# Sliding-window attention and an MLP on one core: the overflow guard's flag is summed where its counts land, without an order behind the residual add of tile 22

## The chip, the cores and the metric

One core of a Trainium2 chip runs the whole kernel. The metric is the time of one launch on the device in microseconds (us), the median of the runs shown. The engines that matter are TensorE (PE, with PEld for its weight loads), VectorE (DVE), ScalarE (ACT), GpSimd (POOL) and SyncE (SP). A name with a q behind it in the profile (POOLq, SPq) is that engine's sequencer: it loads registers, branches, waits on semaphores and issues DMAs.

## The reference

Inputs are q, k and v of 4 batches, 8 heads, 768 positions and 64 values per head, in float32. Cut to what matters:

```python
scores = q @ k.T / 8
keep = (column < 4) | ((0 <= row - column) & (row - column < 128))   # 4 sinks, a window of 128
a = softmax(where(keep, scores, -1e9))
x = (a @ v), heads side by side                    # (4, 768, 512)
xn = (x - mean) / sqrt(var + 1e-6) * g_ln
out = x + relu(xn @ w_ch1) @ w_ch2                 # 512 -> 2048 -> 512
```

## The kernel before

The 4 x 768 rows are 24 tiles of 128 rows (`NT = 24`), and two tiles make a chunk of 256 rows (`NC = 12`). A chunk's attention gives `x`, which is normalised, transposed by a DMA that SP issues (L598), multiplied by `w1` (`mlp`, matmuls on L1070), put through a ReLU on ACT (L1081), and multiplied by `w2`. From chunk 3 on the second product is done block by block with seven products of halves instead of eight (`second_by_seven`, matmuls on L1122); for this DVE makes sums and differences of halves of the hidden layer (L1098, tiles named `sb` and `natc`). The last chunk, tiles 22 and 23, has its own code (`last_by_seven`): its DVE additions are on L1174 and its stores on L1179. The names of those additions in the code are k11, k21, k22, o11, o21, o22, k12 and o12; the table `tail["sum", t]` keeps, for a tile, one operation of its residual sum. For tile 22 (`NT - 2`) that is the operation named o21.

The softmax is done without subtracting the maximum. A guard says whether that was allowed. On DVE it clamps the reciprocals of all sums, compares the clamped ones with the originals and counts, for each of the 128 partitions, how many differ (L1285 to L1287, into `n_bad`). A DMA that POOL issues (L1291, `gmove`) turns the column of 128 counts into a row on one partition (`n_bad_t`). DVE then sums the row (L1295, into `n_sum`) and converts the sum to an integer (L1296, into `flag`); these two instructions are the operation `gflag`. At the end each of the five engines loads `flag` into a register (L1335) and branches on it (L1337): where it is zero, each jumps over a slow general version of the whole computation (`general`). After the branch stands the end of the program (shown under L1372): the engines wait for what is outstanding, meet at a barrier that POOL collects, clear the semaphores, and meet once more.

What sets the order is a planner (`Plan`). Every operation is given with its engines and assumed costs, the buffers that it reads and writes, and a priority (a smaller number goes first). `Plan.run` goes through an imagined time, and on each engine it starts the operation with the best priority among those that could start within a short window; the instructions are written out in the order of those start times. `after=[...]` makes an operation start only when the listed ones have ended. `gflag` has priority 1000, behind all other work of DVE. The last store on SP (`order_last`) is kept back and written behind SP's load of the flag, the other engines' loads of the flag stand behind everything else that they do:

```python
bad = nc.values_load(flag, min_val=0, max_val=128 * NT * H)
order_last.emit(order_last.eng)
```

Two operations named `hold` and `hold_act` (L1299, L1302) make PE and ACT read the last output value before they load the flag.

Of the kernel before, what the change touches and what calls it, by code (L numbers as in the profile page):

```python
# [213 lines left out]
def fix(occ, extra=0.09):  # L214
    return (occ, occ + extra)
# [159 lines left out]
def kernel(  # L375
# [23 lines left out]
    NT = B * RB  # L399
# [8 lines left out]
    P = Plan()  # L408
# [110 lines left out]
    def negs(e):  # L519
# [18 lines left out]
         writes=[gr_b], dma=HW_T)  # L538
    P.op("gtt", pe(0.1), PAR["gtt"], lambda e: nc.tensor.transpose(gt_p.t[:, 0:NDM], g_rows, ident_f[0:NDM, 0:NDM]),
         reads=[gr_b, Bc["ident_f"]], writes=[gt_p])  # L540
    P.op("gtc", {"DVE": fix(0.07)}, PAR["gtt"] + 0.1, lambda e: V.tensor_copy(gt, gt_p.t[:, 0:NDM]), reads=[gt_p], writes=[Bc["gt"]])
    for h in range(H):
# [3 lines left out]
            reads=[Bc["vc"]], writes=[Bc["vcd"]], nb=3.5 + 0.55 * h)  # L546
    for b in range(B):
# [4 lines left out]
            reads=[Bc["vcd"], Bc["vc"], Bc["sel4" if b else "sel"]], writes=[Bvs[b]], nb=PAR["vs0"][1] if b == 0 else PAR["vs1"] if b == 1 else 40.0 * b)  # L552
# [8 lines left out]
    for c in range(4):  # L561
        for n in range(len(Bw1[c])):
# [3 lines left out]
                 writes=[Bw1[c][n]], dma=half_w if len(Bw1[c]) > 1 else SW_W)  # L566
    for c in range(4):
        P.op(f"w2ld{c}", {"POOL": (0.75, 0.8)}, PAR["w2p"][c], lambda e, c=c: G.dma_start(
            w2[c], moe_w_ch2[512 * c:512 * (c + 1), :].rearrange("(t p) n -> p t n", p=128)),
            writes=[Bw2[c]], dma=SW_W)  # L570
# [674 lines left out]
    last_use, tail = {}, {}  # L1245
# [19 lines left out]
    for n, (in0, in1, op, reads) in enumerate((  # L1265
# [4 lines left out]
        for m in range(2):  # L1270
            P.op(f"w2t{n}{m}", {"DVE": dve(1024, 0.64), "POOL": (2.1, 2.2)} if PAR["w2t_pool"] else {"DVE": dve(1024, 0.64)}, 16.0 * PAR["seven"] + PAR["w2t"] + 0.5 * n + 0.1 * m,
                 lambda e, n=n, m=m, in0=in0, in1=in1, op=op: (V if e == "DVE" else G).tensor_tensor(w2t[n][m], in0(m), in1(m), op=op),
                 reads=[Bw2[m], Bw2[m + 2], *reads], writes=[Bw2t[n]], after=natf_users if n < 2 else natp_users)
    for c in range(NC):
        mlp(c)
        if c == PAR["x_by_dma"] - 1:
            for s in range(4):
                for j in range(NDM):
# [3 lines left out]
                         reads=[*Bw1[s], Bc["gt"]], writes=[Bw1g[s]], after=last_use[s])  # L1282

    def guard(e):
# [3 lines left out]
    nb_b, fl_b = Buf("n_bad"), Buf("flag")  # L1288
    P.op("guard", {"DVE": fix(0.9)}, 1000.0, guard, reads=recs, writes=[nb_b])
    nt_b = Buf("n_bad_t")  # L1290
    P.op("gmove", {"POOL": (0.8, 0.85)}, 1000.0, lambda e: G.dma_start(n_bad_t[0:1, :], n_bad[:, 0:1]),  # L1291
         reads=[nb_b], writes=[nt_b], dma=SW_Q)

    def total(e):
        V.tensor_reduce(out=n_sum, in_=n_bad_t, op=ALU.add, axis=mybir.AxisListType.X)  # L1295
        V.tensor_copy(flag, n_sum)  # L1296
    P.op("gflag", {"DVE": fix(0.2)}, 1000.0, total, reads=[nt_b], writes=[fl_b], after=[tail["sum", NT - 2]])
    hl = Buf("hold", "one")
    P.op("hold", pe(0.06), 1000.0, lambda e: nc.tensor.matmul(  # L1299
        hl.t[0:1, 0:1], lhsT=tail["ot"].t[:, tail["at"]:tail["at"] + 1], rhs=ones_f, start=True, stop=True),  # L1300
        reads=[tail["ot"], tail["oo"], Bc["ones_f"]], writes=[hl])
    P.op("hold_act", {"ACT": act(1)}, 1001.0, lambda e: nc.scalar.copy(act_end, tail["ot"].t[0:1, tail["at"]:tail["at"] + 1]),  # L1302
         reads=[tail["ot"], tail["oo"]], writes=[Buf("hold_act")])
# [73 lines left out]
```

## Time and profile before

| | us |
|---|---|
| median of 3 runs | 209.81 |
| lowest and highest run | 209.40 and 209.91 |
| the profiled execution's own time | 209.76 |
| its span, first to last instruction | 208.2 |
| PE busy in the span | 201.3 (97%) |
| DVE busy in the span | 160.7 (77%) |
| POOL busy in the span | 115.7 (56%) |

Between the span and the time of the profiled execution lie 1.56 us, before the first and behind the last instruction that the trace shows. Positions are given in us from the start of the span. PE's granted clock is full in all 40 slices of the page. Rows that group instructions by line give the smallest, median and longest duration in nanoseconds, and then the start of the first and of the last instruction of the group.

### The profile page before, as it was taken

Reading aid. Unit: us, or ns where it says so; the run is one execution under the profiler, and the core shown is the slowest. Engines: PE = TensorE matmul, PEld = TensorE weight load, DVE = VectorE, ACT = ScalarE, POOL = GpSimd, SP = SyncE. Lnnn points to the kernel's source line nnn. Section 1 sums busy time; section 2 is a strip of 40 time slices with the busy share of each in tenths; the row PEclk is TensorE's granted clock in tenths of the full one; section 3 lists DMA queues with packets and bytes.
Section 4 is the critical chain, followed back from the end, with each engine's and each line's share of the span. In section 5 each row is a group of like instructions: output and inputs, shape, how many; then the busy total and the mean of one; then the engine's idle time right before and its main releaser. Section 6 shows DMA issues by size and latency. Waiting matters only on the chain.

```text
span 208.2 us, 7258 instructions
## 1 busy us (share of the span) xinstructions
PE 201.3 (97%) x2987; PEld 169.9 (82%) x2987; DVE 160.7 (77%) x434; ACT 120.8 (58%) x216; POOL 115.7 (56%) x170
## 2 busy tenths in 40 slices
PE   7798999999999999999999999999999999999993
PEld 2457985688889888888888888888888888888892
DVE  5599764899948889888788788888788788772483
ACT  3798786343675499575565564565564564463520
POOL 7969842479799794848767666567442022320000
PEclk9999999999999999999999999999999999999999
DMA  5999999999999799999999999999997310310403
GB/s 151 191 186 199 190 205 206 172 181 148 141 201 130 74 184 156 76 196 160 82 203 125 104 196 125 107 199 107 124 187 61 126 28 5 126 28 0 104 13 98
DMA packets 103789, 27.56 MB, mean 132 GB/s; under 512 B 92740, under 2 KB 100936, under 8 KB 103752
## 3 DMA queue, kind: packets, MB, share of 16 engines
q0 software_dynamic: 70960, 13.18, 90.9%
q1 hardware_dynamic: 31448, 13.09, 35.8%
q10 hardware_dynamic: 1344, 0.79, 1.3%
q8 instruction: 24, 0.39, 0.9%
q14 instruction: 13, 0.11, 0.2%
HBM read 27.43 MB, written 6.29 MB: 162 GB/s over the span
## 4 chain that ended last, share of the span: by engine, by line
PE 91%; DVE 3%; DMA 3%; ACT 1%; issue 1%; ACTq 0%
PE one L1070 41%; PE one L1122 27%; PE one L1228 10%; PE pair L1011 3%; DMA natf<-in_q_dram 3%; PE one L984 2%; PE one L991 2%; PE one L1000 1%; PE one L927 1%; PE pair L1019 1%; DVE st L905 1%; DVE x L897 1%; PE pair L626 1%; PE pair L754 1%; PE one L882 0%
## 5 line engine op out<-in xcount | busy, mean ns | idle before, releaser
L1070 PE MATMUL one<-xnt,w 128*128 128x256 bf16 x768 | 88.5, 273 | 0.3 <-issue 0.3
L1070 PEld LDWEIGHTS <-w 128*128 128x128 bf16 x768 | 74.0, 98 | 10.0 <-issue 0.5
L1081 ACT ACTIVATE h<-one 128x512 bf16<-128x512 f32 x86 | 51.3, 598 | 35.9 <-PE one L1070 34.3
L667 POOL DMA_DIRECT2D vn<-in_v_dram x59 | 39.2, 689 | 8.3 <-DMA w<-in_moe_w_ch_dram 7.1
L1029 ACT ACTIVATE pe<-pair 128x768 bf16<-128x768 f32 x36 | 27.2, 809 | 16.5 <-PE pair L1011 16.0
L915 POOL TENSOR_SCALAR st<-st 128x1 f32<-128x1 f32 x24 | 9.6, 401 | 48.0 <-DVE st L907 47.6
L1122 PEld LDWEIGHTS <-h 128*128 128x128 bf16 x224 | 21.4, 98 | 2.6 <-issue 0.2
L1228 PE MATMUL one<-w,h 128*128 128x256 bf16 (+1 forms) x160 | 22.9, 294 | 0.0
L1228 PEld LDWEIGHTS <-h 128*128 128x128 bf16 x160 | 15.1, 98 | 4.6
L1122 PE MATMUL one<-w,h 128*128 128x256 bf16 (+1 forms) x152 | 18.8, 267 | 0.0
L1122 PEld LDWEIGHTS <-sb 128*128 128x128 bf16 x176 | 16.9, 98 | 2.2
L1129 ACT COPY tx<-one 128x256 f32<-128x256 f32 x24 | 9.0, 375 | 16.2 <-PE one L1122 16.2
L916 POOL TENSOR_TENSOR st<-st,mhalf 128x1 f32<-128x1 f32 x24 | 16.6, 691 | 2.0
L905 DVE BATCH_NORM_STATS2 st<-x 128x6 f32<-128x512 bf16 x24 | 16.7, 694 | 0.8
L1163 DVE TENSOR_TENSOR ot<-ot,x 128x512 f32<-128x512 f32 x15 | 10.4, 692 | 7.6 <-ACT ot L1129 7.4
L1054 DVE TENSOR_TENSOR x<-one,rec 128x256 bf16<-128x256 f32 x36 | 15.2, 422 | 1.1
L727 POOL DMA_DIRECT2D nat<-in_k_dram x16 | 14.9, 935 | 1.4 <-DMA natp<-in_q_dram 1.4
L727 POOL DMA_DIRECT2D nat<-in_q_dram x16 | 14.4, 910 | 0.0
L919 DVE TENSOR_SCALAR xc<-x,st 128x512 bf16<-128x512 bf16 x18 | 7.4, 412 | 7.5 <-POOL st L916 7.5
L1122 PE MATMUL one<-natf,sb 128*128 128x256 bf16 x92 | 12.5, 273 | 0.0
L1034 DVE TENSOR_TENSOR pe<-pe,band 128x768 bf16<-128x768 bf16 x24 | 11.9, 538 | 0.0
L1122 PEld LDWEIGHTS <-natc 128*128 128x128 bf16 x112 | 10.6, 98 | 1.4
(148 smaller groups left out, 304.7 us busy)
## 6 DMA issues: line engine op xcount, KB each, us to landing
out_dram<-ot SPq DMA_DIRECT2D x20, 256.0 KB
w<-in_moe_w_ch_dram POOLq DMA_DIRECT2D x6, 512.0 KB, 12.3
nat<-in_k_dram POOLq DMA_DIRECT2D x16, 128.0 KB, 4.7
nat<-in_q_dram POOLq DMA_DIRECT2D x16, 128.0 KB, 5.6
vn<-in_v_dram POOLq DMA_DIRECT2D x44, 32.0 KB, 4.8
w<-in_moe_w_ch_dram POOLq DMA_DIRECT2D x4, 256.0 KB, 11.2
vn<-in_v_dram POOLq DMA_DIRECT2D x15, 64.0 KB, 4.3
natp<-in_k_dram POOLq DMA_DIRECT2D x3, 256.0 KB, 12.1
```

Source lines behind the costliest of these rows:

```text
L667: P.op(f"vld{t}_{i}", {"POOL": (0.8, 0.85)}, prio + 0.001 * i, lambda e, p0=p0, n=n, hs=hs, src=src: G.dma_start(m.t[p0:p0 + n, hs, 0:64], ...
L727: lambda e, nat=nat, ap=ap: G.dma_start(nat.t, ap), writes=[nat], dma=SW_N, after=gate(c), nb=PAR["k_nb"].get((c, nm, i), 0.0))
L905: P.op(f"bn{t}", {"DVE": fix(0.60)}, d + 0.12, lambda e: V.bn_stats(st.t[:, 8:14], x.t), reads=[x], writes=[st, mv])
L916: G.tensor_tensor(st.t[:, 16:17], st.t[:, 17:18], mhalf, op=ALU.pow)),
L1029: nc.scalar.activation(pes[j].t.rearrange("p a b -> p (a b)")[:, 0:768].rearrange("p (a b) -> p a b", a=2), pps[j].t[:, :, 0:384], AF.Exp, ...
L1034: V.tensor_mul(at_s, at_s, band[j] if r > 1 else edge[r][j].unsqueeze(1).to_broadcast([128, 4, 192]))
L1054: P.op(f"x{t - 1}{u}", {"DVE": dve(256)}, d + 0.051 + 0.002 * u, lambda e, u=u, rc=rc, pv=pv: V.tensor_tensor(x.t[:, 256 * u:256 * u + 256 ...
L1070: nc.tensor.matmul(ph.t[:, 256 * s:256 * s + 256], lhsT=w1[ht // 4][:, j, 128 * (ht % 4):128 * (ht % 4 + 1)], rhs=xnt.t[:, j, :], start=j ...
L1081: nc.scalar.activation(dst, ph.t, AF.Relu)
L1122: nc.tensor.matmul(bank.t[:, 0:n], lhsT=left[p](m)[:, a, :], rhs=right[p](m)[:, a, cols], start=new and m + a == 0, stop=m + a == 4, skip_ ...
L1163: V if e == "DVE" else G).tensor_tensor(ot[i].t, ot[i].t, x.t, op=ALU.add), reads=[ot[i], *oo[i], x], writes=[done])
L1228: nc.tensor.matmul(pc.t[:, part], lhsT=h1[s].t[:, 256 * ii + 128 * i:256 * ii + 128 * i + 128], rhs=w2[s][:, ii, sl.start + part.start:sl. ...
```

## The change

The operation `gflag` loses its `after`. Nothing else is edited.

```diff
     def total(e):
         V.tensor_reduce(out=n_sum, in_=n_bad_t, op=ALU.add, axis=mybir.AxisListType.X)
         V.tensor_copy(flag, n_sum)
-    P.op("gflag", {"DVE": fix(0.2)}, 1000.0, total, reads=[nt_b], writes=[fl_b], after=[tail["sum", NT - 2]])
+    P.op("gflag", {"DVE": fix(0.2)}, 1000.0, total, reads=[nt_b], writes=[fl_b])
```

The planner puts the two instructions elsewhere on DVE; on PE, ACT, POOL and SP every instruction stands where it stood. In the rows below a name is a tile with its number, the last figure is partitions x elements.

On DVE, in the middle of chunk 10's second product, among the sums of halves of its hidden layer, the flag's two instructions come in:

```order
@@ -397,4 +397,6 @@
 L1098 TENSOR_TENSOR sb_158<-natc_70,h_150 128x512
 L1098 TENSOR_TENSOR sb_160<-h_152,sb_158 128x512
+L1295 TENSOR_REDUCE n_sum<-n_bad_t 1x1
+L1296 CAST flag<-n_sum 1x1
 L1098 TENSOR_TENSOR natc_72<-h_151,h_153 128x512
 L1098 TENSOR_TENSOR sb_159<-natc_72,h_151 128x512
```

They now stand ahead of the sums that use the hidden halves `h_151` and `h_153`. On DVE, near the end, in the last chunk's additions (`tx` and `ot` are its partial sums and output tiles), they go:

```order
@@ -419,6 +421,4 @@
 L1174 TENSOR_TENSOR tx_167<-one_65,tx_167 128x256
 L1174 TENSOR_TENSOR ot_171<-one_64,tx_167 128x256
-L1295 TENSOR_REDUCE n_sum<-n_bad_t 1x1
-L1296 CAST flag<-n_sum 1x1
 L1174 TENSOR_TENSOR ot_171<-one_65,tx_166 128x256
 L1174 TENSOR_TENSOR tx_164<-one_65,x_122 128x256
```

Behind o21 (`ot_171<-one_64,tx_167`) now comes o22 (`ot_171<-one_65,tx_166`) at once, and then k12.

## The prediction

> **What bounds the kernel now.** I read the page's head first, then its chain of waits, and then, since the edit touches a few tenths of a microsecond, the instructions in order of time around the old and the new place and every row of the program's end.
>
> ```profile
> span 208.2 us, 7258 instructions
> PE 201.3 (97%) x2987; PEld 169.9 (82%) x2987; DVE 160.7 (77%) x434; ACT 120.8 (58%) x216; POOL 115.7 (56%) x170
> PE 91%; DVE 3%; DMA 3%; ACT 1%; issue 1%; ACTq 0%
> ```
>
> The second line is the busy time of the engines, the third the chain that ended last, by engine. TensorE is the bound. An edit on DVE counts only where PE waits for DVE, or behind PE's last product, where the end is made. The profiled execution took 209.76 us, 0.05 under the median of 209.81, so a difference found in its trace is taken off the median as it stands.
>
> The last chunk's end in order of time (start, duration, engine, line):
>
> ```profile
> 202.50 0.42 DVE L1174 TENSOR_TENSOR ot<-one,tx 128x256 f32<-128x256 f32 x1 [0.45 <-PE one L1122]
> 202.73 0.60 PE L1122 MATMUL one<-natf,sb 128*128 128x256 bf16 x4
> 202.84 0.26 DVE L1295 TENSOR_REDUCE n_sum<-n_bad_t 1x1 f32<-1x128 f32 x1
> 202.95 2.39 SPq L1179 DMA_DIRECT2D out_dram<-ot  x2
> 203.13 0.14 DVE L1296 CAST flag<-n_sum 1x1 int32<-1x1 f32 x1
> 203.37 0.42 DVE L1174 TENSOR_TENSOR ot<-one,tx 128x256 f32<-128x256 f32 x1
> 203.60 0.60 PE L1122 MATMUL one<-w,natc 128*128 128x256 bf16 x4
> 204.04 0.61 PE L1122 MATMUL one<-w,h 128*128 128x128 bf16 x8
> 204.24 0.74 DVE L1174 TENSOR_TENSOR ot<-one,tx 128x256 f32<-128x256 f32 x2
> ```
>
> The flag's two instructions run from 202.84 to 203.27. The addition behind them, o22 at 203.37, uses the product whose last matmul ends at 202.73 + 0.60 = 203.33. The two additions at 204.24 follow products that end at 204.20 and 204.65, and the last output is ready at 204.24 + 0.74 = 204.98. So DVE waits for PE here, and the flag lies in that wait.
>
> Now the flag's way out. These are its loads by POOL, SP and ACT, then POOL's steps behind its branch, each group with its duration in ns and its first and last start:
>
> ```profile
> L1335 POOLq TENSOR_LOAD <-flag x1: 502/502/502, 203.3 to 203.3; - x1
> L1335 SPq TENSOR_LOAD <-flag x1: 529/529/529, 203.3 to 203.3; - x1
> ...
> L1335 ACTq TENSOR_LOAD <-flag x1: 498/498/498, 205.1 to 205.1; - x1
> ```
>
> ```profile
> L1337 POOLq EVENT_SEMAPHORE  x5: 17/43/43, 204.4 to 204.7; - x5
> L1337 POOLq COMPARE_BRANCH  x1: 59/59/59, 203.9 to 203.9; - x1
> L1337 POOLq INC_SWDGE_SEM  x1: 632/632/632, 204.8 to 204.8; - x1
> ```
>
> And the end of the program up to the first barrier, which POOL collects, with the release of SP behind it from a later cut of the same view:
>
> ```profile
> L1372 SPq EVENT_SEMAPHORE  x11: 28/28/28, 206.0 to 206.7; - x11
> L1372 SPq DRAIN  x2: 7/10/13, 206.8 to 206.8; - x2
> L1372 POOLq DRAIN  x1: 1865/1865/1865, 205.5 to 205.5; - x1
> L1372 DVEq DRAIN  x1: 17/17/17, 206.0 to 206.0; - x1
> L1372 PEldq DRAIN  x1: 8/8/8, 206.2 to 206.2; - x1
> L1372 ACTq DRAIN  x1: 8/8/8, 206.3 to 206.3; - x1
> L1372 POOLq EVENT_SEMAPHORE  x1: 17/17/17, 207.4 to 207.4; - x1
> ```
>
> ```profile
> L1372 SPq EVENT_SEMAPHORE  x2: 17/17/17, 207.5 to 208.1; - x2
> ```
>
> This is what the chain of waits does not show, since it ends with ACT's last copy. DVE, PE and ACT are through at 206.0, 206.2 and 206.3, SP at 206.8. POOL is last: its drain runs from 205.5 for 1.865 us, its wait for the others ends at 207.4 without waiting for any of them, and SP is let go at 207.5. POOL had nothing else to do since the counts' DMA at 182.93. Its way is flag written at 203.27, load 203.3 to 203.8, branch 203.9, semaphores from 204.4, the counter instruction of 0.632 at 204.8, drain, 207.4: 4.1 us behind the flag. The other four depend on the last output at 204.98 instead. So the flag, by way of POOL, sets the end.
>
> **The change part by part.** *The old place on DVE.* 0.26 + 0.14 and the 0.03 between them, 0.43 us of work, goes. o22 still has to wait for the product that ends at 203.33, and its 203.37 stays; so do the two last additions and 204.98. Worth 0 on the path; late next is PE, as before.
>
> *The new place on DVE.* It is in chunk 10's second product. The rows around it, with the DMA that brings the counts, the ReLU that DVE waits for and the products that follow:
>
> ```profile
> 182.93 0.66 POOL L1291 DMA_DIRECT2D n_bad_t<-n_bad  x1 [0.26 <-DVE n_bad L1287]
> 185.25 0.42 DVE L1098 TENSOR_TENSOR sb<-h,sb 128x512 bf16<-128x512 bf16 x1
> 185.46 0.60 ACT L1081 ACTIVATE h<-one 128x512 bf16<-128x512 f32 x1 [0.28 <-PE one L1070]
> 186.09 0.42 DVE L1098 TENSOR_TENSOR natc<-h,h 128x512 bf16<-128x512 bf16 x1 [0.41 <-ACT h L1081]
> 186.54 0.42 DVE L1098 TENSOR_TENSOR sb<-natc,h 128x512 bf16<-128x512 bf16 x1
> 187.00 1.04 PE L1122 MATMUL one<-natf,sb 128*128 128x256 bf16 x8
> 187.88 1.04 PE L1122 MATMUL one<-w,h 128*128 128x256 bf16 x8
> ```
>
> ```profile
> DMA to landing us min/median/max: 2.0/2.0/2.0
> ```
>
> The counts land 2.0 us after 182.93, at 184.9, 0.7 us before DVE gets there. The sum needs nothing of the instruction ahead of it, and as at 202.50 and 202.84 it can start 0.34 behind that one's start: 185.59, converted by 186.02. Then DVE waits for the ReLU, which ends at 185.46 + 0.60 = 186.06, and goes on at 186.09 as before: the cover is DVE's idle 0.41. If the sum starts only when the work ahead ends (185.67), it is done at 186.10 and the next addition slips by some 0.05. Behind it in DVE's queue stand `natc` and `sb`; `sb` is ready at 186.96 and feeds the second half of the product that starts at 187.00, that is its fifth matmul, at 187.00 + 4 x 0.11 = 187.44 (eight take 187.88 - 187.00). That leaves 0.44 more. With all cover gone the cost would be the whole 0.43, which still fits in it. I take 0, with 0 to 0.43 as bounds.
>
> *SP.* Its flag load cannot move: the store ahead of it is issued at 202.95 and an issue takes 0.342,
>
> ```profile
> L1179 SPq DMA_DIRECT2D out_dram<-ot x3: 332/342/348, 201.3 to 205.0; - x3
> ```
>
> so SP comes to the flag at 203.29 and already loads it at 203.3. Its last store, at 205.0, waits for the output of 204.98. SP's arrival stays at 206.8. DVE, PE and ACT load the flag behind their last work, as before: 0.
>
> *POOL.* With the flag at 186.0 instead of 203.27, POOL's whole way starts 17.2 us earlier: load 186.1, drain from 188.2, at the barrier by 190.2, some 16 us ahead of everyone. It is queued behind nothing, and nobody waits for it until the barrier. Then SP is last, at 206.8. POOL's wait would end there plus the time in which a semaphore passes between engines; the release at 207.5 behind the 207.4 bounds that at 0.1. So the end comes forward by 207.4 - 206.8 - 0.1 = 0.5. Upper bound: SP's whole wait at this barrier, the longest in this row, less nothing:
>
> ```profile
> SPq L1372 <- PEq L1372: 1.2, 2, 0.7
> ```
>
> Lower bound: 0, if the drain's 1.865 us does not move. I take 0.5, since all other steps of POOL's way have durations of their own and only that one is open.
>
> The sum: 0 + 0 + 0 - 0.5. 209.81 - 0.5 = 209.31; for the profiled execution a span of 207.7 and 209.26.
>
> **The rivals.** *B: POOL's drain is tied to the end, and nothing changes.* For it: the drains of the other engines take 8 to 17 ns, POOL's a hundred times that, so it may be a wait for something of the end. In the last 2.5 us the instruction queue moves 4 of the 13 packets of the execution:
>
> ```profile
> q14 instruction: 4, 0.03, 5.0%
> ```
>
> ```profile
> q14 instruction: 13, 0.11, 0.2%
> ```
>
> If POOL's drain waits for such a fetch, and the fetch for what the other engines do once they have the flag, the drain would end at 207.4 in any case: 209.8. Against it: POOL passes its own branch at 203.9, 1.2 us before ACT loads the flag, and the drain follows an instruction that took 0.632 on POOL alone. The Trainium skill ("VectorE: DVE Perf Modes", The DRAIN you can't avoid) says that drains of the start and end code are constant, about 12 ns, on all five engines. By that rule POOL's 1865 ns would be no work of its own, and case B would give 209.8; the rows of four engines agree with it and POOL's does not, so I leave it the smaller chance.
>
> *C: the counts land late and DVE stalls ahead of PE's operands; slower.* DVE is in order, and the three sums behind the flag would wait for the DMA. With a landing at L, the sum starts at L + 0.04, the next addition at L + 0.52 instead of 186.09; with the 0.44 of room PE loses L - 186.01. Set against the 0.5 at the end, the kernel gets slower once the landing comes 3.6 us after the issue, and by over 0.3% at 4.2 us. The landing in this trace took 2.0. POOL's other DMAs take longer, under load and with 64 times the bytes:
>
> ```profile
> vn<-in_v_dram POOLq DMA_DIRECT2D x44, 32.0 KB, 4.8
> ```
>
> At 4.8 us L is 187.73, PE loses 1.7, and the time is 209.81 + 1.7 - 0.5 = 211.0. Against it: POOL issues no load behind 182.93, so the queue is empty.
>
> *D: the cover at the new place fails altogether and the end does not move.* 0.43 more, 210.24, still within 0.3% of before.
>
> **How the numbers follow.** About 0.3% (0.63 us) is what a measurement of this kernel can tell from no change. Case A, the forecast, has 0.71; B 0.14; C 0.09; D 0.06. A's gain lies between 0.4 and the 0.7 of SP's wait, and the runs shown spread by 0.5 us, so I give a third of A to a gain over 0.63: 0.24, and with a little of B's scatter 0.25. Within 0.3%: the rest of A, B and most of D, 0.64. Slower: C and a part of D, 0.11. The range runs from 209.81 - 0.7 less 0.15 of scatter, 208.95, to B's median with the upper half of the spread, 209.95; it leaves out C and D. A alone spans 209.0 to 209.55.
>
> **What would show it.** Right: POOL's flag load near 186.1 and its 1.865 us drain near 188; POOL's barrier wait ending within 0.1 of SP's last drain, at 206.9; DVE's `natc` still at 186.09 and o22 at 203.37; a span near 207.7. Wrong for case A: a POOL drain that lasts to 207.4 or is stretched over the 17 us, or an SP that arrives later than 206.8 because its last store lands later. Wrong for the zero at the new place: a DVE gap ahead of L1295 that ends with the counts' DMA, and PE idle before 187.44.

## The result, and the profile after

The changed kernel takes 209.05 us (median of 9 runs, 208.91 to 209.49), the kernel before 209.64 us (9 runs, 209.31 to 209.95). The ratio is 0.9976, with a 95% interval of 0.9965 to 0.9987: 0.5 us, or 0.24%, faster.

The profiled execution of the changed kernel took 209.49 us, the highest of its runs. The head of its page and its chain of waits:

```profile
span 208.0 us, 7258 instructions
PE 202.2 (97%) x2987; PEld 170.5 (82%) x2987; DVE 161.2 (77%) x434; ACT 120.8 (58%) x216; POOL 115.8 (56%) x170
PE 90%; DVE 4%; DMA 2%; ACT 1%; issue 1%; SPq 0%; ACTq 0%; DVEq 0%
```

The span is only 0.2 us shorter than before, because this execution lost 0.33 us long before the edit: compared matmul by matmul, the two traces are 0.01 us apart at the 500th, at 38.7 us, and 0.31 to 0.34 from the 600th, at 45.7, to the end. So positions here are to be read 0.33 to 0.34 us later than the same work before. The new place, in order of time:

```profile
183.27 0.66 POOL L1291 DMA_DIRECT2D n_bad_t<-n_bad  x1 [0.26 <-DVE n_bad L1287]
185.59 0.42 DVE L1098 TENSOR_TENSOR sb<-h,sb 128x512 bf16<-128x512 bf16 x1
185.93 0.27 DVE L1295 TENSOR_REDUCE n_sum<-n_bad_t 1x1 f32<-1x128 f32 x1
186.24 0.14 DVE L1296 CAST flag<-n_sum 1x1 int32<-1x1 f32 x1
186.42 0.42 DVE L1098 TENSOR_TENSOR natc<-h,h 128x512 bf16<-128x512 bf16 x1
187.34 1.04 PE L1122 MATMUL one<-natf,sb 128*128 128x256 bf16 x8
```

The sum starts 0.34 us behind the start of the instruction ahead of it, the flag is written at 186.38, and `natc` follows at 186.42, which is the 186.09 of before plus the shift. The row of the product still has its eight matmuls in 1.04 us. The old place, with the last output:

```profile
203.70 0.42 DVE L1174 TENSOR_TENSOR ot<-one,tx 128x256 f32<-128x256 f32 x1 [0.45 <-PE one L1122]
204.58 0.74 DVE L1174 TENSOR_TENSOR ot<-one,tx 128x256 f32<-128x256 f32 x2
```

o22 at 203.70 is the 203.37 of before plus the shift: where the flag's 0.43 us stood, DVE now idles 0.45 us until PE is ready. POOL's load of the flag and its steps behind it, and the end up to the first barrier:

```profile
L1335 POOLq TENSOR_LOAD <-flag x1: 502/502/502, 186.4 to 186.4; - x1
...
L1335 SPq TENSOR_LOAD <-flag x1: 532/532/532, 203.7 to 203.7; - x1
```

```profile
L1372 SPq DRAIN  x2: 7/10/13, 207.1 to 207.2; - x2
L1372 POOLq EVENT_SEMAPHORE  x2: 17/17/17, 207.2 to 207.3; - x2
L1372 POOLq DRAIN  x1: 1865/1865/1865, 188.6 to 188.6; - x1
L1372 DVEq DRAIN  x1: 17/17/17, 206.4 to 206.4; - x1
L1372 PEldq DRAIN  x1: 8/8/8, 206.6 to 206.6; - x1
L1372 ACTq DRAIN  x1: 8/8/8, 206.6 to 206.6; - x1
```

POOL's drain has moved to 188.6 and still takes 1.865 us. SP's last drain, at 207.2, is now the last to arrive, and POOL sees it at 207.2. From the last output to the end of the span it is 208.0 - 205.32 = 2.7 us; before it was 208.2 - 204.98 = 3.2. The 0.33 us lost early and this 0.5 make up the whole difference of the spans: 208.16 + 0.33 - 0.50 = 207.99.

### The profile page after: what moved, and what is told of

The parts are those of the page before. It is cut to its first block, busy times and chain, and to the rows that moved or that the text cites. A ratio compares the mean times of both kernels' runs of the same rounds, so it can differ in the third digit from the quotient of the medians.

```text
span 208.0 us, 7258 instructions
## 1 busy us (share of the span) xinstructions
PE 202.2 (97%) x2987; PEld 170.5 (82%) x2987; DVE 161.2 (77%) x434; ACT 120.8 (58%) x216; POOL 115.8 (56%) x170
## 4 chain that ended last, share of the span: by engine, by line
PE 90%; DVE 4%; DMA 2%; ACT 1%; issue 1%; SPq 0%; ACTq 0%; DVEq 0%
PE one L1070 41%; PE one L1122 27%; PE one L1228 10%; PE pair L1011 3%; DMA natf<-in_k_dram 2%; PE one L984 2%; PE one L991 2%; PE one L1000 1%; DVE st L905 1%; DVE x L897 1%; PE one L927 1%; PE pair L1019 1%; DVE xc L912 1%; PE pair L626 1%; ACT natc L695 1%
```

## The experiments

Theory A is the prediction's: the flag sets the end by way of POOL, some 4.1 us of POOL's own steps behind it, and with the flag early SP sets the end. Rivals are B (POOL's drain is tied to the end) and R, which the size of the gain suggests: DVE is rid of 0.43 us among its last additions, and that is the gain. Each ratio below is to the kernel before, run on the same chip.

### e1: the changed kernel again

The edit is that of the change.

> The changed kernel once more, against which the others of this group are read. Theory A (the flag sets the end by way of POOL: flag, then 4.1 us of POOL's own steps, and from there the barrier; without it SP's arrival sets the end): 0.5 us faster than before, ratio 0.9976, and from the last output to the end of the span 2.7 us instead of 3.2. Rival R (the 0.43 us of work that DVE no longer does among the last additions is the gain): the same 0.4 to 0.5 us, but with the last output that much earlier after PE's last product, and 3.2 us behind it as before.

Measured: 209.16 us against 209.77, ratio 0.9972 (0.9962 to 0.9982). In its trace the last output is at 205.16 and the span ends at 207.84: 2.7 us. That is A's figure.

### e2: the flag one addition earlier

```diff
+        tail["k21d"] = o6            # in last_by_seven, behind k21d
-    ... reads=[nt_b], writes=[fl_b], after=[tail["sum", NT - 2]])
+    ... reads=[nt_b], writes=[fl_b], after=[tail["k21d"]])
```

> The flag stays among the last chunk's additions on DVE, but one addition earlier: behind k21d, ahead of o21, where DVE idles 0.45 us. By A it is written near 202.4 instead of 203.27, POOL arrives near 206.5, ahead of SP's 206.8, and the whole gain is there: 0.5 us faster than before, equal to the changed kernel within 0.1 us. By R the 0.43 us still lie among the last additions, so nothing is gained: ratio 1.000. If the new place of the changed kernel cost something hidden, this one would be faster than the changed kernel by that.

Measured: 209.08 us, ratio 0.9972 (0.9962 to 0.9981), the same as e1. The flag among the last additions, and then the first barrier (in this kernel the lines from the edit on count one more):

```profile
201.44 0.42 DVE L1174 TENSOR_TENSOR tx<-one,tx 128x256 f32<-128x256 f32 x1
201.78 0.26 DVE L1296 TENSOR_REDUCE n_sum<-n_bad_t 1x1 f32<-1x128 f32 x1
202.08 0.14 DVE L1297 CAST flag<-n_sum 1x1 int32<-1x1 f32 x1
202.31 0.42 DVE L1174 TENSOR_TENSOR ot<-one,tx 128x256 f32<-128x256 f32 x1
203.19 0.42 DVE L1174 TENSOR_TENSOR ot<-one,tx 128x256 f32<-128x256 f32 x1 [0.45 <-PE one L1122]
```

```profile
L1373 POOLq DRAIN  x1: 1865/1865/1865, 204.4 to 204.4; - x1
L1373 SPq DRAIN  x2: 7/10/13, 206.6 to 206.7; - x2
```

The whole gain is there with the flag's 0.43 us still among the last additions, so R falls. POOL is done at 204.4 + 1.9 = 206.3, 0.4 us ahead of SP. The flag, at 202.22, came 4.1 us ahead of that. Against the last output (204.80 here, 204.98 before) the flag is 0.87 us earlier than before. That one addition is all that the gain needs; the other 16 us by which the change moves the flag are worth nothing.

### e3: the flag last

```diff
-    ... after=[tail["sum", NT - 2]])
+    ... after=[tail["o22"]])        # o22 recorded in last_by_seven; the planner puts the flag behind everything
```

> The flag is the last work of DVE, behind the last output: it is written near 205.35, 2.1 us later than before. SP's last store stands behind SP's load of the flag and so is issued near 206.3 instead of 205.0, and SP arrives near 208.2. By A POOL arrives 4.1 us behind the flag, at 209.45, and the kernel is 2.05 us slower than before (211.7, ratio 1.010). If POOL's drain is tied to the end or to the other engines (B), the end follows SP instead: 208.2 against 207.4, 0.8 us slower (ratio 1.004). By R: SP's delay alone, 0.8 us or less.

Measured: 212.37 us, ratio 1.0127 (1.0108 to 1.0146), 2.6 us slower, more than either expected. The first barrier in its trace:

```profile
L1372 SPq EVENT_SEMAPHORE  x12: 27/28/28, 207.7 to 209.8; - x12
L1372 SPq DRAIN  x2: 7/10/13, 209.8 to 209.9; - x2
L1372 POOLq DRAIN  x1: 1865/1865/1865, 207.8 to 207.8; - x1
```

The flag was written at 205.44, and POOL's drain ended at 207.8 + 1.9 = 209.6: again 4.2 us behind it, as A has it. But SP arrived later still, at 209.9. Its last store went out at 206.5, where 206.3 was expected; its waits then took from 207.7 to 209.8, where before they took from 205.9 to 206.7. The last of these waits is for the landing of that store, which the trace puts at 209.76: 3.3 us behind its issue, instead of 1.7 (205.0 to 206.68) before. So the run does not tell A from B by its time, only by the place of POOL's drain, and what stretched that landing is open. Two things are seen there: all five engines loaded the flag at 205.5 and branched between 206.1 and 206.9, and the store's 144 DMA packets took from 207.34 to 208.96 (before from 205.92 to 206.34), with five packets of the instruction queues moving between 207.22 and 208.43. Before, no such packet moved beside the store's. That either is the cause is not shown.

### e4 and e5: ballast on POOL, in the kernel before and in the changed one

```diff
         bad = nc.values_load(flag, min_val=0, max_val=128 * NT * H)
+        for _ in range(4):
+            G.tensor_tensor(low, rec, rec, op=ALU.mult)
         order_last.emit(order_last.eng)
```

> The kernel before, with four extra additions of 128x192 elements on POOL alone behind its load of the flag; their result is used by nothing, DVE, PE, ACT and SP do what they did. From the 1.15 us of a 128x512 one, each is estimated at 0.4 to 0.5 us, so four take 1.6 to 2.0 and end near 205.7; the first of POOL's waits at the end, at 204.4, is for its own work, so POOL's way gets some 1.1 to 1.6 us longer. A: 1.1 to 1.6 us slower than before (ratio 1.005 to 1.008). B and R: no change, 1.000, as POOL would not set the end.

> The same four extra additions on POOL, behind its load of the flag, in the changed kernel. POOL has some 16 us to spare there. A: nothing, the ratio to before stays 0.9976. If POOL's arrival still mattered: slower than the changed kernel by 1.1 to 1.6 us, ratio to before 1.003 to 1.005. The four run at 187 to 189 beside DVE's sums; if POOL's work slowed DVE there, PE would have 0.44 us of room.

Measured: e4 takes 211.25 us against 209.77, ratio 1.0078 (1.0063 to 1.0094), 1.5 us slower. e5 takes 209.22 against 209.63, ratio 0.9978 (0.9969 to 0.9988), the changed kernel's ratio. e4's ballast and first barrier:

```profile
L1337 POOL TENSOR_TENSOR low<-rec x4: 498/507/507, 203.7 to 205.4; 128x192 f32<-128x192 f32 x4
```

```profile
L1374 SPq DRAIN  x2: 7/10/13, 207.8 to 207.8; - x2
L1374 POOLq EVENT_SEMAPHORE  x2: 17/17/17, 209.0 to 209.1; - x2
L1374 POOLq DRAIN  x1: 1865/1865/1865, 207.1 to 207.1; - x1
```

Work on POOL alone, of use to nobody, comes out as time of the kernel before: POOL set its end. In e4's trace POOL's way from its load of the flag to the end of its drain is 1.9 us longer (203.05 to 208.95, before 203.31 to 207.33), and the end of the span is 1.9 us further behind the last output (5.1 us, before 3.2); by the medians it is 1.5 us, by the interval 1.3 to 2.0. SP was not left quite as it was: its last store went out on time, but its waits at the end start only at 207.0, about where POOL's counter instruction ends (206.42 + 0.64). SP is still done at 207.8, 1.1 us ahead of POOL. In the changed kernel the same work costs nothing. B falls with e4 and e5 together: the drain starts and ends with POOL's own steps (207.1 to 209.0 here, 189.9 in e5), and it takes 1865 ns in every trace of this study.

### e6 and e7: the counts later

```diff
+    def move(e):
+        for _ in range(2):           # e7: range(6)
+            G.tensor_tensor(low, rec, rec, op=ALU.mult)
+        G.dma_start(n_bad_t[0:1, :], n_bad[:, 0:1])
-    P.op("gmove", ..., lambda e: G.dma_start(n_bad_t[0:1, :], n_bad[:, 0:1]), ...)
+    P.op("gmove", ..., move, ...)
```

> The changed kernel with two of those additions on POOL ahead of the DMA that brings the counts: its issue comes about 0.9 us later, the landing L at about 185.8 (positions as in the trace of before). By the formula for case C (PE loses L - 186.01 us, when above zero) nothing is lost: ratio to before 0.9976, but DVE now waits for the counts, some 0.2 us. If DVE's order gave less room than reckoned: up to 0.4 us of the gain is gone, ratio up to 0.9995.

> The same with six additions: the DMA 2.7 us later, L at about 187.6. By the formula for case C PE loses L - 186.01 = 1.6 us ahead of the second half of the product that uses sb, and the kernel is 1.6 - 0.5 = 1.1 us slower than before (ratio 1.005). If the loss were made good later (PE's products are followed by the last chunk's first layer, which does not use DVE's sums), it would be smaller or nothing: ratio 0.9976.

Measured: e6 209.50 us against 209.63, ratio 0.9993 (0.9975 to 1.0011), an interval that holds the whole gain as well as none; e7 212.41, ratio 1.0119 (1.0068 to 1.0170), single runs from 211.29 to 213.43. The additions on POOL were slower than estimated: the issue came at 184.13 in e6 and at 186.35 in e7. In e6 the counts also took 2.3 us to land instead of 2.0. Rows of e6, and then of e7:

```profile
185.38 1.04 PE L1122 MATMUL one<-w,h 128*128 128x256 bf16 x8
186.44 0.28 DVE L1300 TENSOR_REDUCE n_sum<-n_bad_t 1x1 f32<-1x128 f32 x1 [0.65 <-DMA n_bad_t<-n_bad]
187.12 1.23 PE L1122 MATMUL one<-natf,sb 128*128 128x256 bf16 x8
187.26 0.42 DVE L1098 TENSOR_TENSOR sb<-natc,h 128x512 bf16<-128x512 bf16 x1
```

```profile
185.08 1.04 PE L1122 MATMUL one<-w,h 128*128 128x256 bf16 x8
185.43 0.61 DVE L1098 TENSOR_TENSOR sb<-h,sb 128x512 bf16<-128x512 bf16 x1
186.35 0.66 POOL L1295 DMA_DIRECT2D n_bad_t<-n_bad  x1
188.38 0.27 DVE L1300 TENSOR_REDUCE n_sum<-n_bad_t 1x1 f32<-1x128 f32 x1 [2.34 <-DMA n_bad_t<-n_bad]
189.68 1.03 PE L1122 MATMUL one<-natf,sb 128*128 128x256 bf16 x4 [2.25 <-DVE sb L1098]
190.50 1.91 PE L1122 MATMUL one<-w,h 128*128 128x256 bf16 x8
```

In e6 DVE waits 0.65 us for the counts, and the product that uses `sb` takes 1.23 us instead of 1.04: PE lost 0.19, and the trace's last output is later by as much. The prediction's formula for case C is in positions of before, where the product ahead starts at 185.25; here it starts at 185.38, 0.13 later, and the sum starts 0.04 behind the landing, so the sum's start of 186.44 means a landing at 186.27 there, and L - 186.01 = 0.26. In e7 the sum starts at 188.38, the shift is -0.17, L is 188.51, and the formula gives 2.5; PE idled 2.25. So the formula holds within 0.25 us for what PE loses there, the room for the counts is 1.1 to 1.3 us, and the loss is not made good later. e7 lost more than its idle time: 20 matmuls from 189.68 to 193.54 took 3.86 us where 20 x 0.11 = 2.2 is usual. The granted clock of that stretch (its columns: PE, PEld, DVE, ACT and POOL busy with counts, then the clock, DMA share and GB/s):

```profile
189.60:194.60 5.00, 4.92 (x30) 3.71 (x31) 1.27 (x4) 0.74 (x2) 0.00 (x0) 0.66 0.00 2
```

The 0.66 is a mean over 5 us: the trace's clock records show half the clock from 189.72 for 3.41 us, and the full clock on both sides. Those 3.41 us at half the clock are the other 1.7 us that the idle time of 2.25 us cost. Not every execution shows this: the profiled one took 213.05 us and another 213.43, both with a mean clock of 0.99, while the two that took 211.29 and 211.77 show 1.00.

### e8: what sets the end now

```diff
-            elif o is not order_last:
+            else:
                 o.emit(o.eng)
         bad = nc.values_load(flag, min_val=0, max_val=128 * NT * H)
-        order_last.emit(order_last.eng)
```

> The changed kernel, but SP issues its last store ahead of its load of the flag instead of behind it; the store itself goes out at the same time, since it waits for the last output. A: SP is the last to arrive now, so its load of 0.53 us and the two register steps behind it, some 0.85 us in all, now lie behind the store's issue and in the path. SP arrives near 207.7 instead of 206.8 (positions as in before), the end is 0.85 us later than the changed kernel's, 0.3 us slower than before: ratio 1.0015. If the landing of the last store or another engine set the end, with SP's steps hidden behind it, the ratio stays 0.9976.

Measured: 209.99 us against 209.71, ratio 1.0019 (1.0008 to 1.0029), 0.4 us slower than before and so 0.9 slower than the changed kernel. SP's load and its arrival:

```profile
L1335 SPq TENSOR_LOAD <-flag x1: 582/582/582, 205.3 to 205.3; - x1
```

```profile
L1371 SPq EVENT_SEMAPHORE  x12: 27/28/28, 206.8 to 207.5; - x12
L1371 SPq DRAIN  x2: 7/10/13, 207.5 to 207.6; - x2
```

The load of the flag, now behind the last store, comes out as time. SP sets the changed kernel's end, and holding its last store back behind the flag is worth 0.9 us there. No version was found that beats the changed kernel: e1, e2 and e5 equal it. In its trace the last of SP's waits starts at 207.05, 0.16 us behind the one ahead of it where the earlier ones follow each other by some 0.06, and the last store lands at 207.04: SP waits some 0.1 us for that landing, which the last output ties to PE. In e8 the store lands at 206.57 and SP's waits run on to 207.5, so there SP's own steps alone set the end.

## Why the prediction was right, step by step

*The old place, 0.* Right: o22 and the last outputs stand where they stood against PE, with DVE idle in place of the flag. e2, which leaves the flag's work among the additions, gains as much.

*The new place, 0.* Right: `natc` and the product behind it kept their places, the cover being DVE's wait for the ReLU. e2 against e1 (209.08 and 209.16) shows no hidden cost of the new place beyond the 0.2 us by which each can be off. The room behind it was reckoned as 0.44 us; e6 and e7 bear out the formula built on it.

*SP, DVE, PE and ACT, 0.* Right: their loads stand behind their last work as before.

*POOL, -0.5.* Right in mechanism and size. The term was the whole of the forecast, 209.31 on a median of 209.81; measured is -0.5 by the ratio, and in the trace 3.2 us from the last output to the end became 2.7. The lower bound of 0 rested on POOL's drain being a wait for the end. It is not: it moved with the flag and kept its 1865 ns. The rule of the Trainium skill that spoke for this (VectorE: DVE Perf Modes, The DRAIN you can't avoid: about 12 ns, on all five engines) fits the 7 to 17 ns of the other four engines and not POOL. It is stated there of the runtime's own code ahead of and behind a kernel, and these drains stand under a line of the kernel; whether it is meant for them is open.

*The rivals.* B fell in e4 and e5. C's mechanism exists, and e7 shows it 2.5 us slower than before; for a wait that long the formula is too low where PE's clock falls behind it, of which it knows nothing: it gives 2.5 - 0.5 = 2.0 us slower for e7, that is 211.6, which lies between the two executions at full clock; the median with the other two is 2.5 slower. In the change itself the counts land 2.1 us behind their issue, at 185.33, with 0.6 us to spare ahead of the sum. D's cost did not arise.

*The chances.* The 0.24% gained is within the 0.3% that had the largest chance, and the time lies in the range, in its lower part. Of the 0.26 us by which 209.05 is under the forecast of 209.31, 0.17 is the kernel before, whose median is 209.64 on nine runs and was 209.81 on the three shown; the rest is within the spread of the runs. So the size of the gain is what bears the forecast out.

## What to carry to other kernels

The end of a program is a barrier, and whoever arrives last sets its time; the chain of waits followed back from the last instruction of work does not name that engine, so the last rows of every queue are to be read against each other. A flag that an engine needs only to leave has a deadline: here POOL's 4.1 us before SP's arrival, and one addition earlier was enough. The same small work is free or costs its full length by which engine it is on and how far that engine is from being the last, which a ballast on that engine alone shows in one run.

## What the runs showed of the hardware that was not expected

- POOL's way from a written flag to the barrier takes 4.1 to 4.2 us in the kernel before, e2 and e3, of which one drain is 1865 ns in each trace. What POOL does in it stays open.
- Where five engines load the flag at the same time (e3), each load takes 597 to 628 ns instead of 483 to 543 in the other runs (582 on SP in e8), and the store behind it lands after 3.3 us instead of 1.7.
- While POOL runs additions of 128x192 elements, three of DVE's four 128x512 sums take 0.59 to 0.61 us instead of 0.42 (e7, the row at 185.43). The fourth, which starts at 183.11 just ahead of a POOL addition, keeps its 0.41, and that addition takes 767 ns, the longest of the row below, against 498 to 507 in e4.
- PE idle for 2.25 us in e7 was followed by 3.41 us at half the clock (a mean of 0.66 over 189.6 to 194.6), and the matmuls of that stretch took up to 417 ns instead of 272, as in the second row. Two of e7's four executions show no lower clock.

The two rows are from the view of e7 by line (smallest, median and longest duration in ns):

```profile
L1294 POOL TENSOR_TENSOR low<-rec x6: 506/566/767, 182.5 to 185.8; 128x192 f32<-128x192 f32 x6
...
L1122 PE MATMUL one<-w,h x8: 417/417/417, 190.5 to 192.0; 128*128 128x256 bf16 x8
```
